# Chunk 2's keys and queries staged during chunk 0's second layer: other rooms, two turns, three loads in flight, chunk norms behind the sums

## The chip, the core and the metric

The kernel runs on one core of a Trainium2 chip. The core has a matrix engine (PE in the profile, its weight loads PEld), three engines for elementwise work (DVE, ACT, POOL), and a sequencer, SP, that does little but issue DMAs. Each engine works through its own list of instructions in order, and waits on semaphores for what other engines or DMAs produce. The metric is the device time of one execution in microseconds (us); lower is better.

## The reference

Inputs are q, k, v of shape (B=4, H=8, S=768, D=48), beta of shape (4, 8, 768), and two weights. Per batch and head a state of 48x48 is carried through the 768 tokens (the delta rule), and the result goes through a two-layer network with SiLU:

```python
k_n = k / (norm(k) + 1e-06)
for t in range(S):
    y[t]  = q[t] @ state
    v_old = k_n[t] @ state
    state = state + beta[t] * outer(k_n[t], v[t] - v_old)
x   = y.transpose(0, 2, 1, 3).reshape(B * S, H * D)      # 3072 x 384
h   = x @ w_in                                           # 384 -> 2048
out = (h * sigmoid(h)) @ w_out                           # 2048 -> 384
```

## The kernel before

**Chunks.** The 768 tokens are cut into 6 chunks of 128 (`NCH`, `C`), and all 32 pairs of batch and head go through a chunk together. Inside a chunk the recurrence becomes a triangular system. For each chunk `c` the kernel makes, in this order:

- `lengths(c)`: the norms of the keys. POOL squares them (`z`, L422), DVE sums the squares (`ss`, L426) and takes a root in a few steps (L441 to L457).
- `load_blocks` (L189): for chunks 2 to 5 it fetches keys and queries from DRAM once more, in blocks of 32 tokens, six DMAs for one half of the batches (G0 or G1) of keys or of queries. `run_rooms` says into which stretch of which other tile: a room that is free at that time. `turn_blocks` (L539, called by `turn_all`) transposes the blocks on DVE into `kq`.
- `spread` (L473, DVE) and `pg` (L496, PE), which put scales of the norms where they are wanted.
- `score` (L580): PE multiplies keys with keys and keys with queries (`pa`), and `ap` takes it out of PSUM, by ACT (L595) and by DVE with a mask (L590). `block_out` and `block_in` take the keys' part of `ap` to DRAM and back in another layout: `blocks<-ap`, then `g<-blocks`.
- `invert(c)`: 31 steps of two instructions on DVE (`rank` L686, `x` L691) and one scaling (L694) invert the 32x32 diagonal blocks. `g<-x`, `low`, `up`, `xe` and `xi` carry the result, partly through DRAM, to `merge` (L840), which puts blocks together on PE (`py`, `px`); `crosses` are its off-diagonal parts.
- `solve(c)`: `ph` (L886, keys on the state), `pz` and `pyc` (L898, L966, L979), `pu` (L918), `state<-state,pu` (L925, DVE). `even_heads` copies the attention's output out of PSUM into `xT`: for odd heads into `part` first, from which DMAs bring it to `xT` (L959).

**The layer.** `xT` is multiplied by `w_in` (`phid`, L1109), goes through SiLU into `gT`, and is multiplied by `w_out`: for chunk 0 by `project` (`po`, L1252, results in `o` and `rest`), for the others by `combine` (`px`/`py`, L1326), which saves products by working on sums of chunks' tiles (`sums_of_g`, L1306, DVE) and of the weights (`sums_of_w`). From chunk 2 on the first product saves some too (`hx`, `hu`, L1163). `run()` issues the next item of the layer.

**What sets the order.** The order on every engine is that of the program text: `pin` ties each instruction to the one pinned before it on its engine, and `in_line` (L104) does so for the DMAs that SP issues. So one waiting instruction holds all that stand behind it on its engine. Ahead of chunk 2 the text is a string of words that `script` reads, one word a step and a number of repeats: `s` a step of `solve`, `r` an item of the layer, `f` a fetch of weights, `t` a step of the sums of `w_out`, `m` a step of chunk 2's norms, `K`, `L`, `y` loads and turns of chunk 2, `c` what is left of chunk 0's layer and the start of chunk 1's. From chunk 2 on, plain loops order the work: `paced` puts steps of `invert` between items of the layer by a balance of estimated times, `run_to` issues items up to a count, and `go(after, n)` puts in n steps of the next chunk's norms.

**Holding back loads.** `linked` lets the first DMA of a call wait for the last one issued ahead of it. `deep(fetch, ..., n=2)` lets each load of a call wait until the n-th load ahead of it has landed, so that n are in flight. `load_blocks` was not called through either.

Of the kernel before, what the change touches and what calls it, by code (L numbers as in the profile page):

```python
# [19 lines left out]
def kernel(  # L20
# [11 lines left out]
    B, H, S, D = q.shape  # L32
    DM, DFF = moe_w_in.shape
    P = 128
# [3 lines left out]
    NP = H // 2  # L38
    BH = B * H
    W = 64  # L40
# [127 lines left out]
    def run_rooms(c):  # L168

        n = HB * NP * RUN  # L170
        ap = ap0s[:].rearrange("p g u h t -> p (g u h t)")
        late = spare_s if c == 2 else halves[int(c == 3)]
        for j, g, of, i in ((0, 0, ap, 0), (0, 1, late, 0), (1, 0, late, 1), (1, 1, halves[0] if c == 2 else ap, 0)):
            runs[c, j, g] = of[:, n * i : n * (i + 1)].rearrange("p (n r) -> p n r", r=RUN)
# [19 lines left out]
    def in_blocks(c):  # L194

        return 1 < c < NCH
# [172 lines left out]
    xis = [xi[:, g] for g in range(2)]  # L369
    crosses = {1: spare_s[:, 0 : HH * T].rearrange("p (n t) -> p n t", t=T)}  # L370

# [662 lines left out]
    def solve(c):  # L1034
# [34 lines left out]
        for hf in range(2):  # L1069
# [7 lines left out]
            for g in range(2):  # L1077
                together(inner(c, g, hf), old(c, g, hf))
            if hf == 1 and c == 1:
                load_blocks(q, 2, G1)  # L1080
            elif hf == 1 and in_blocks(c + 1):
                turn_all(c + 1, 1, G0)
# [212 lines left out]
    def group(g):  # L1295
        return slice(FG * g, min(FG * (g + 1), NFF // 2))

    def sum_g(c, hf, which, fs):
        k, left, right, op = which
        fs = group(fs) if isinstance(fs, int) else fs  # L1300
        of = [
            sums_of_g[:, x, fs] if isinstance(x, int) else
            gT[:, home(c, hf), fs, x[0] * GT + x[1] * C : x[0] * GT + (x[1] + 1) * C]
            for x in (left, right)
        ]
        pin(nc.vector.tensor_tensor(out=sums_of_g[:, k, fs], in0=of[0], in1=of[1], op=op))  # L1306
# [329 lines left out]
    def prepare(c):  # L1636
# [42 lines left out]
    sizes_1 = [0, 1]  # L1679
    sums_made = sum_w()  # L1680
    later = {}

    def script(text):

        nonlocal pieces
        for word in text.split():
# [63 lines left out]
    for text in (  # L1750
        "s f s f T f q T s q T j5 j4 j8 j8 f j5 f q r T j20 j5 j8 j4 j16 j5 j4 b r q r f j4 j4 f W7 r b j4 f2 j4 j4 j32 r f e j6 j6 b j8 j4 f j4 j20 f j4 r j4 j99 l h f2 b l s w2 f r2 l p r s l w3 r p r l p f l2 f l3 b l f l2 s l f l p l3 r l3 s l f l r l2 p f s2 l2 H f l4 f r2 f p2 v l g G r i p i p r2 f i i2 r i r i b l i r f r i r b r2 i b b b i2 r2 i2 f b i5 r6 f r f r i2 r2 f r i r f r f i4 f i b r2 i3 b f b f r i r i f k r f r z i b r s r2 t z s b r2 b s m2 r5 t f t m f t m2 r s t m r b s b m r m2 s K r m L r m r c m2 s y m r m t b m2 s m2 b m f m2 t r t m3 r m s m",
    ):
# [24 lines left out]
    go(after, 99)  # L1777

# [11 lines left out]
    def paced(steps, first):  # L1790
# [81 lines left out]
```

## Time and profile before

| | |
|---|---|
| runs | 649.12, 646.27, 642.19 us; median 646.27 |
| the profiled execution | 653.0 us |
| its span, first to last instruction | 651.3 us |
| mean granted clock of PE | 0.965 of full speed |
| PE busy | 623.3 us (96% of the span) |
| DVE busy | 441.2 us (68%) |
| ACT, POOL busy | 238.8 us (37%), 97.6 us (15%) |
| DMA | 55.07 MB, mean 85 GB/s |

All times of the trace count from the first instruction. The profiled execution is 1.7 us longer than its span, which is what lies around it, and 6.7 us longer than the median of the runs. "Busy" is the time in which an engine works on an instruction. PE's busy time alone doesn't say how much work was done, since the profile also gives the clock that PE was granted, and at half the clock the same products take twice as long. A row of the timeline gives start, duration, engine, line, operation and, in brackets, how long the engine stood idle ahead of it and what ended that. PE's rows in the trace have two records for a product that the program's order has once.

### The profile page before, as it was taken

How to read it: one execution, taken by the hardware profiler on the slowest of the kernel's cores; microseconds unless marked ns; L12 is line 12 of the kernel's file. 1: busy time of each engine (PE TensorE's matmuls, PEld its weight loads, DVE VectorE, ACT ScalarE, POOL GpSimd, SP SyncE). 2: the span in 40 equal slices, each digit the busy share in tenths (PEclk: the TensorE clock that was granted, in tenths of full speed). 3: DMA queues.
4: the chain of work that ended last, by engine and by line, in shares of the span. 5: the costliest groups of instructions: out<-in, count | busy, mean ns of one | idle time of the engine just before them, and what ended most of it. 6: DMA issues, size and time to landing. Idle time of an engine off the chain costs nothing.

```text
span 651.3 us, 21911 instructions
## 1 busy us (share of the span) xinstructions
PE 623.3 (96%) x9570; PEld 544.5 (84%) x9570; DVE 441.2 (68%) x946; ACT 238.8 (37%) x542; POOL 97.6 (15%) x99
## 2 busy tenths in 40 slices
PE   8889899999969998999999999999999999999997
PEld 5678788666658986889898998898998899998997
DVE  5755779998486967577888577986769855231332
ACT  3565655152242122453422443431443324434211
POOL 5433531245000031000050000040000020000000
PEclk9768999999978996999999999999999999999999
DMA  7755554150766129126234546066333060110011
GB/s 152 185 129 170 160 129 98 49 147 3 131 123 123 32 74 173 34 64 129 46 73 78 123 92 134 20 107 130 83 80 73 1 107 13 41 26 0 1 25 25
DMA packets 143936, 55.07 MB, mean 85 GB/s; under 512 B 113488, under 2 KB 137296, under 8 KB 143840
## 3 DMA queue, kind: packets, MB, share of 16 engines
q1 hardware_dynamic: 143360, 53.00, 37.9%
q8 instruction: 75, 1.23, 0.8%
q10 hardware_dynamic: 480, 0.67, 0.4%
q14 instruction: 21, 0.17, 0.1%
HBM read 40.99 MB, written 10.49 MB: 79 GB/s over the span
## 4 chain that ended last, share of the span: by engine, by line
PE 50%; DVE 2%; ACT 1%; POOL 1%; issue 1%; DMA 1%; SPq 0%; DVEq 0%; POOLq 0%; ACTq 0%
PE px L1326 12%; PE hu L1163 12%; PE hx L1163 10%; PE py L1326 9%; PE pz L898 1%; PE ph L886 1%; PE pyc L979 1%; PE pyc L966 1%; PE pa L580 1%; PE pu L918 1%; DVE kq L539 1%; PE py L840 1%; PE px L840 1%; POOL z L422 1%; DMA g<-blocks 1%
## 5 line engine op out<-in xcount | busy, mean ns | idle before, releaser
L1109 PE MATMUL phid<-xT,w_in 128*128 128x256 f32 x384 | 95.7, 403 | 1.0 <-issue 0.9
L1109 PEld LDWEIGHTS phid<-xT,w_in 128*128 128x128 f32 x384 | 74.5, 200 | 13.2 <-issue 2.3
L1326 PE MATMUL px<-sums_of_w,sums_of_g 128*128 128x192 f32 x320 | 57.3, 329 | 1.1 <-DVE sums_of_g L1306 1.1
L1326 PE MATMUL py<-w_out,sums_of_g 128*128 128x192 f32 x320 | 57.4, 329 | 0.0
L1306 DVE TENSOR_TENSOR sums_of_g<-gT 128x512 f32<-128x512 f32 (+2 forms) x44 | 30.7, 734 | 36.9 <-PE py L1326 18.8
L686 DVE SCALAR_TENSOR_TENSOR rank<-g,step,x 128x31 f32<-128x31 f32 (+15 forms) x124 | 49.7, 401 | 7.9 <-DMA g<-blocks 5.0
L1326 PEld LDWEIGHTS px<-sums_of_w,sums_of_g 128*128 128x128 f32 x320 | 52.2, 190 | 2.1 <-ACT o L1367 1.3
L1326 PEld LDWEIGHTS py<-w_out,sums_of_g 128*128 128x128 f32 x320 | 52.2, 190 | 0.5
L1163 PE MATMUL hx<-xT,w_in 128*128 128x256 f32 x192 | 48.0, 379 | 0.0
L691 DVE TENSOR_TENSOR x<-x,rank 128x31 f32<-128x31 f32 (+15 forms) x124 | 42.5, 343 | 4.3
L1163 PE MATMUL hu<-xT,w_in 128*128 128x256 f32 x192 | 45.4, 379 | 0.0
L1163 PEld LDWEIGHTS hu<-xT,w_in 128*128 128x128 f32 x192 | 36.5, 190 | 5.0
L1163 PEld LDWEIGHTS hx<-xT,w_in 128*128 128x128 f32 x192 | 36.4, 190 | 4.8
L1178 DVE TENSOR_TENSOR gT<-gT,hx 128x512 f32<-128x512 f32 x32 | 21.9, 684 | 26.7 <-PE hx L1163 26.4
L1337 DVE TENSOR_TENSOR o<-o,kept 128x192 f32<-128x192 f32 (+1 forms) x29 | 12.4, 426 | 39.8 <-ACT kept L1334 39.4
L580 PE MATMUL pa<-kq 48*64 48x128 f32 (+1 forms) x768 | 26.6, 292 | 6.2 <-ACT xT L595 4.1
L580 PEld LDWEIGHTS pa<-kq 48*64 48x64 f32 x768 | 22.9, 159 | 10.7 <-ACT xT L595 4.9
L595 ACT COPY xT<-pyc 48x128 f32<-48x128 f32 (+2 forms) x120 | 31.1, 259 | 1.6
L925 DVE TENSOR_TENSOR state<-state,pu 48x384 f32<-48x384 f32 x44 | 24.3, 552 | 8.9 <-PE pu L918 7.9
L595 ACT COPY gT<-hu 128x512 f32<-128x512 f32 x32 | 18.7, 585 | 30.6 <-PE hu L1163 30.6
L601 POOL COPY g<-x 64x256 f32<-64x256 f32 x4 | 3.8, 938 | 174.0 <-DVE x L694 174.0
L1326 PE MATMUL py<-w_out,gT 128*128 128x192 f32 x160 | 28.8, 330 | 0.3 <-issue 0.3
(233 smaller groups left out, 1212.6 us busy)
## 6 DMA issues: line engine op xcount, KB each, us to landing
vf<-in_v_dram SPq DMA_DIRECT2D x48, 96.0 KB, 3.7
out_dram<-o SPq DMA_DIRECT2D x42, 96.0 KB, 2.2
w_out<-in_moe_w_in_dram SPq DMA_DIRECT2D x12, 256.0 KB, 3.7
sums_of_w<-in_moe_w_out_dram SPq DMA_DIRECT2D x8, 384.0 KB, 4.2
blocks<-ap SPq DMA_DIRECT2D x40, 64.0 KB, 1.9
g<-blocks SPq DMA_DIRECT2D x4, 512.0 KB
up<-x SPq DMA_DIRECT2D x4, 512.0 KB, 4.2
xi<-up SPq DMA_DIRECT2D x16, 128.0 KB, 3.4
```

The costliest lines, as they stand in the source:

```text
L580: pin(nc.tensor.matmul(pa[e][half, p * n * W : (p + 1) * n * W], lhsT=kq[rows, p, 0, half], rhs=kq[rows, p, js[0] : js[-1] + 1, half], sta ...
L595: return pin(nc.scalar.copy(to, of))
L686: pin(nc.vector.scalar_tensor_tensor(out=tv, in0=g[:, 0:m, m : m + 1].to_broadcast([P, m, n]), scalar=step[:, m : m + 1], in1=x[:, m : m + ...
L691: yield pin(nc.vector.tensor_tensor(out=x[:, 0:m, m:T], in0=x[:, 0:m, m:T], in1=tv, op=ALU.add))
L840: yield pin(nc.tensor.matmul(pm[to, T * n : T * (n + 1)], lhsT=left, rhs=right, start=True, stop=True))
L925: pin(nc.vector.tensor_tensor(out=to, in0=to, in1=by_heads(pu[of]), op=ALU.add))
L1109: pin(nc.tensor.matmul(ph[:, j * GT : (j + 1) * GT], lhsT=w_in[:, a, (2 * f + j) * P : (2 * f + j + 1) * P], rhs=xTs[c, hf][:, a, :], star ...
L1163: pin(nc.tensor.matmul(to[:, GT * i : GT * (i + 1)], lhsT=weights[:, f], rhs=moving, start=start and i == 0, stop=True, skip_group_check=True,
L1178: return lambda: pin(nc.vector.tensor_tensor(out=at(fs, j, hf), in0=at(fs, j, hf), in1=of(room), op=ALU.add))
L1306: pin(nc.vector.tensor_tensor(out=sums_of_g[:, k, fs], in0=of[0], in1=of[1], op=op))
L1326: pin(nc.tensor.matmul(to, lhsT=at, rhs=quarter(f, *b) if isinstance(b, tuple) else sums_of_w[b][:, f], start=start and n == 0, stop=n == ...
L1337: pin(nc.vector.tensor_tensor(out=to, in0=to, in1=of, op=ALU.add))
```

## The change

It has four parts.

1. **Chunk 2's loads.** The keys of the second half of the batches (G1) and the queries of the first (G0) are now fetched (`L`) directly behind the last fetch of `w_out`, the keys of G0 (`K`) and the queries of G1 (the new word `J`, into a room in `sums_of_g` in place of one in `gT`) soon after. All go through `deep(..., n=3)`. The room of `crosses[1]` moves from `spare_s` to `ap0`, behind the runs that lie there.
2. **Turns and scores.** `y1` turns keys and queries of G0, `y2` those of G1. Norms, spread, scores (`P`, `o`), the sums of `w_in` (`u`) and the load of the values (`V`) are now words of the script, the scores with an item of the layer between batches where the words say so.
3. **Invert of chunk 2.** It is no longer issued at a fixed beat but by a balance: each item of the layer gives 1.31 less what DVE's sums beside it take (`spent`), each step takes its estimate. Behind it stand four items ahead of `merge`, where six stood.
4. **The loop over chunks 2 to 5.** The loads of the next chunk's keys (G1) and queries (G0) go three deep, those of chunk 3's keys ahead of the loop. The steps of the norms that stood between `invert` and `merge` are moved: one or three stay there, the others come behind the sums and copies of the following step of `solve`. `paced` begins at the fourth item for each chunk, and `run_to` goes two items further, with fewer behind it.

```diff
...
-        for j, g, of, i in ((0, 0, ap, 0), (0, 1, late, 0), (1, 0, late, 1), (1, 1, halves[0] if c == 2 else ap, 0)):
+        last = sums_of_g[:].rearrange("p k f t -> p (k f t)") if c == 2 else ap
+        for j, g, of, i in ((0, 0, ap, 0), (0, 1, late, 0), (1, 0, late, 1), (1, 1, last, 0)):
...
-    crosses = {1: spare_s[:, 0 : HH * T].rearrange("p (n t) -> p n t", t=T)}
+    behind_runs = ap0s[:].rearrange("p g u h t -> p (g u h t)")[:, HB * NP * RUN :]
...
+    crosses = {1: behind_runs.rearrange("p (n t) -> p n t", t=T)}
...
-            if hf == 1 and c == 1:
-                load_blocks(q, 2, G1)
-            elif hf == 1 and in_blocks(c + 1):
+            if hf == 1 and c > 1 and in_blocks(c + 1):
                 turn_all(c + 1, 1, G0)
...
+        spent[0] += 0.17 + 0.13 * (fs.stop - fs.start)
...
         if in_blocks(c):
-            if c == 2:
-                turn_all(c, 1, G0)
-                yield
-            turn_all(c, 1, G1)
-            if c == 2:
-                yield
+            if c > 2:
+                turn_all(c, 1, G1)
             for b in range(B):
                 scored(b)
+                if c == 2 and b < B - 1:
+                    yield
             block_in(c)
...
             elif what == "K":
-                load_blocks(k, 2, G0)
+                deep(load_blocks, k, 2, G0, n=3)
             elif what == "L":
-                load_blocks(k, 2, G1)
-                load_blocks(q, 2, G0)
+                deep(linked, load_blocks, k, 2, G1, n=3)
+                deep(load_blocks, q, 2, G0, n=3)
+            elif what == "J":
+                deep(load_blocks, q, 2, G1, n=3)
             elif what == "y":
-                turn_all(2, 0, ALL)
+                for j in range(2):
+                    turn_all(2, j, (G0, G1)[n - 1])
+            elif what == "P":
+                later["ready"] = prepare(2)
+                later["step"] = block_steps(2)
+            elif what == "o":
+                go(later["ready"], n)
+            elif what == "u":
+                go(sums_in, n)
+            elif what == "V":
+                linked(load_v, 2)
...
-    ready = prepare(2)
-    go(ready)
-    run(1)
-    go(ready)
-    step = block_steps(2)
-    run(1)
-    go(ready)
-    sums_in = sum_w_in()
-    go(sums_in, 6)
-    linked(load_v, 2)
-    run(7)
-    for n, _ in enumerate(invert(2, step)):
-        run(int(n % 4 != 3 and n != 24))
-        if n == 3:
-            load_k(3)
-    for g in range(2):
-        size(2, g)
-    after = lengths(3)
-    for n in range(6):
-        go(after, 6)
-        run()
-    go(after, 99)
+    assert next(sums_made, 0) == 0
...
+    credit, m, left = 0.0, T - 1, True
+    steps = invert(2, later["step"])
+    while left:
+        spent[0] = 0.0
+        run()
+        credit += 1.31 - spent[0]
+        while left and credit > 0.0:
+            left = next(steps, 0) != 0
+            credit -= 0.38 + 0.00225 * m * (T - m) if m > 0 else 1.2
+            m -= 1
+        if m == T - 6:
+            load_k(3)
+    deep(load_blocks, k, 3, G1, n=3)
+    for g in range(2):
+        size(2, g)
+    after = lengths(3)
+    for n in range(4):
+        run()
+        go(after, (1, 1, 1, 0)[n])
...
-            if n == (1 if c == 2 else 2) and more:
-                assert c == 2 or done[0] >= start(c) - OUTPUT - 4
-                load_blocks(k, c + 1, G1)
-            if n == (2 if c == 2 else 3) and more:
-                load_blocks(q, c + 1, G0)
+            if n == 2 and c > 2 and more:
+                assert done[0] >= start(c) - OUTPUT - 4
+                deep(load_blocks, k, c + 1, G1, n=3)
+            if n == (1 if c == 2 else 3) and more:
+                deep(load_blocks, q, c + 1, G0, n=3)
+            if n > 2:
+                go(after, 8)
             if n == 5 and c == 2:
                 go(sums_in, 2)
+        go(after, 99)
...
-        paced(invert(c + 1, step), 4 if c == 2 else 2)
+        paced(invert(c + 1, step), 4)
...
-        run_to(start(c) + ITEMS + 1)
-        for n in range(7 if c == 2 else 4):
-            go(after, (2, 2, 6, 6, 6, 6, 6)[n])
+        run_to(start(c) + ITEMS + 3)
+        for n in range(3 if c == 2 else 2):
+            go(after, 2 - n)
             run()
-        go(after, 99)
+        go(after, 1)
...
```

The words of the script differ at its end only. From the last `z` on they were, and are now:

```
z i b r s r2 t z s b r2 b s m2 r5 t f t m f t m2 r s t m r b s b m r m2 s K r m L r m r c m2 s y m r m t b m2 s m2 b m f m2 t r t m3 r m s m

z i b r s r2 t z s L b r2 b s K m2 r5 t f t m f t m2 r s J t m r b s b m r m2 s r m r m r c m2 s y1 m t r m b r s m3 b f m2 t r m2 r t m2 s y2 m r m3 s P o2 r u r u r o2 V r3 u4
```

**SP, from the last fetch of `w_out` on.** In the rows `x2` counts equal DMAs in a row; `in_k_dram` and `in_q_dram` are the inputs k and q, `ap_83` is the tile `ap0`, `sums_of_w_in` the room `spare_s`. Before:

```order
L334 DMA sums_of_g<-in_moe_w_out_dram 128x768 x2
L959 DMA xT<-part 48x2x128 x2
L959 DMA xT<-part 16x2x128
L959 DMA xT<-part 32x2x128
L959 DMA xT<-part 48x2x128
L189 DMA ap_83<-in_k_dram 32x8x176
...
L189 DMA sums_of_w_in<-in_q_dram 16x8x160 x2
L104 DMA out_dram<-o 64x384 x4
L104 DMA out_dram<-rest 64x384 x4
L189 DMA gT<-in_q_dram 16x8x176 x2
```

And of the change:

```order
L335 DMA sums_of_g<-in_moe_w_out_dram 128x768 x2
L190 DMA sums_of_w_in<-in_k_dram 16x8x176 x2
...
L190 DMA ap_83<-in_k_dram 16x8x160 x2
L190 DMA sums_of_g<-in_q_dram 16x8x176 x2
L190 DMA sums_of_g<-in_q_dram 16x8x160 x2
L190 DMA sums_of_g<-in_q_dram 32x8x176
L190 DMA sums_of_g<-in_q_dram 32x8x160
L962 DMA xT<-part 48x2x128 x2
L962 DMA xT<-part 16x2x128
L962 DMA xT<-part 32x2x128
L962 DMA xT<-part 48x2x128
L104 DMA out_dram<-o 64x384 x4
L104 DMA out_dram<-rest 64x384 x4
```

All 24 loads now stand ahead of the moves from `part` to `xT`. Before, 18 of them stood between those moves and the stores of `o` and `rest`, and 6 behind the stores.

**PE at the merge of chunk 2.** `phid` is the first product of chunk 1's layer, `py<-xe,ap_83` the merge, `ph` the keys on the state. Before:

```order
L1326 MATMUL py<-w_out_109,sums_of_g 128x192 x4
L1326 MATMUL py<-w_out_110,sums_of_g 128x192 x4
L1109 MATMUL phid<-xT,w_in 128x256 x33
L840 MATMUL py<-xe,ap_83 32x32 x64
L1109 MATMUL phid<-xT,w_in 128x256 x3
```

And of the change:

```order
L1330 MATMUL py<-w_out_109,sums_of_g 128x192 x4
L1330 MATMUL py<-w_out_110,sums_of_g 128x192 x4
L1110 MATMUL phid<-xT,w_in 128x256 x27
L843 MATMUL py<-xe,ap_83 32x32 x64
L1110 MATMUL phid<-xT,w_in 128x256 x3
```

The merge has 27 products ahead of it in place of 33, that is two items of the layer fewer.

**DVE behind the invert of chunk 3.** `x<-x,step` is its last instruction, `sums_of_g<-...` are the sums that `px` and `py` of the layer read, `ss`, `seed` and `nt` belong to chunk 4's norms. Before:

```order
L694 TENSOR_TENSOR x<-x,step 128x1024
L598 COPY g<-x 64x32x24
L1306 TENSOR_TENSOR sums_of_g<-gT 128x512 x2
L426 TENSOR_REDUCE ss<-z 128x8 x4
L441 TENSOR_SCALAR seed<-ss 128x32
L1306 TENSOR_TENSOR sums_of_g<-sums_of_g,gT 128x512 x2
L446 TENSOR_SCALAR nt<-ss,seed 128x32
```

And of the change:

```order
L697 TENSOR_TENSOR x<-x,step 128x1024
L601 COPY g<-x 64x32x24
L1310 TENSOR_TENSOR sums_of_g<-gT 128x512 x2
L1310 TENSOR_TENSOR sums_of_g<-sums_of_g,gT 128x512 x2
L429 TENSOR_REDUCE ss<-z 128x8 x4
L444 TENSOR_SCALAR seed<-ss 128x32
L601 COPY y<-py 32x512 x2
```

The second pair of sums now stands ahead of `ss`, and the root's steps behind the copies of `solve`.

More of the change, by code (lines that the diff above doesn't have):

```diff
@@ L369 @@
     xis = [xi[:, g] for g in range(2)]
-    crosses = {1: spare_s[:, 0 : HH * T].rearrange("p (n t) -> p n t", t=T)}
+    behind_runs = ap0s[:].rearrange("p g u h t -> p (g u h t)")[:, HB * NP * RUN :]
+    assert HB * NP * RUN + HH * T == 2 * HB * H * W
+    crosses = {1: behind_runs.rearrange("p (n t) -> p n t", t=T)}
     ALL_ROWS = slice(0, P)
@@ L1296, in group @@
         return slice(FG * g, min(FG * (g + 1), NFF // 2))
+    spent = [0.0]
     def sum_g(c, hf, which, fs):
@@ L1679 @@
     sizes_1 = [0, 1]
-    sums_made = sum_w()
+    sums_made, sums_in = sum_w(), sum_w_in()
     later = {}
@@ L1750 @@
     for text in (
-        "s f s f T f q T s q T j5 j4 j8 j8 f j5 f q r T j20 j5 j8 j4 j16 j5 j4 b r q r f j4 j4 f W7 r b j4 f2 j4 j4 j32 r f e j6 j6 b j8 j4 f j4 j20 f j4 r j4 j99 l h f2 b l s w2 f r2 l p r s l w3 r p r l p f l2 f l3 b l f l2 s l f l p l3 r l3 s l f l r l2 p f s2 l2 H f l4 f r2 f p2 v l g G r i p i p r2 f i i2 r i r i b l i r f r i r b r2 i b b b i2 r2 i2 f b i5 r6 f r f r i2 r2 f r i r f r f i4 f i b r2 i3 b f b f r i r i f k r f r z i b r s r2 t z s b r2 b s m2 r5 t f t m f t m2 r s t m r b s b m r m2 s K r m L r m r c m2 s y m r m t b m2 s m2 b m f m2 t r t m3 r m s m",
+        "s f s f T f q T s q T j5 j4 j8 j8 f j5 f q r T j20 j5 j8 j4 j16 j5 j4 b r q r f j4 j4 f W7 r b j4 f2 j4 j4 j32 r f e j6 j6 b j8 j4 f j4 j20 f j4 r j4 j99 l h f2 b l s w2 f r2 l p r s l w3 r p r l p f l2 f l3 b l f l2 s l f l p l3 r l3 s l f l r l2 p f s2 l2 H f l4 f r2 f p2 v l g G r i p i p r2 f i i2 r i r i b l i r f r i r b r2 i b b b i2 r2 i2 f b i5 r6 f r f r i2 r2 f r i r f r f i4 f i b r2 i3 b f b f r i r i f k r f r z i b r s r2 t z s L b r2 b s K m2 r5 t f t m f t m2 r s J t m r b s b m r m2 s r m r m r c m2 s y1 m t r m b r s m3 b f m2 t r m2 r t m2 s y2 m r m3 s P o2 r u r u r o2 V r3 u4",
     ):
```

## The prediction

> **What bounds the kernel now.** I read the page's head and first part, then PE's waits, then windows around the largest of them, then the timelines of SP, ACT and DVE there.
>
> ```profile
> span 651.3 us, 21911 instructions
> PE 623.3 (96%) x9570; PEld 544.5 (84%) x9570; DVE 441.2 (68%) x946; ACT 238.8 (37%) x542; POOL 97.6 (15%) x99
> ```
>
> PE is busy in 623.3 of 651.3 us, so 28 us of idle time, and stretches at a reduced clock, are all that an edit of the order can win. PE's waits (us in total, times, longest) say for what it idled:
>
> ```profile
> PE pa L580 <- ACT xT L595: 4.1, 1, 4.1
> PE py L840 <- DMA xe<-low: 2.4, 2, 1.6
> ...
> PE pyc L979 <- issue: 1.6, 2, 1.3
> ...
> PE pg L496 <- DVE spread L473: 1.1, 1, 1.1
> PE px L1326 <- DVE sums_of_g L1306: 1.1, 1, 1.1
> ...
> PE phid L1109 <- issue: 0.9, 2, 0.7
> PE pyc L966 <- issue: 0.9, 1, 0.9
> PE pa L580 <- DVE kq L539: 0.8, 2, 0.5
> PE pa L580 <- DVE ap L590: 0.6, 2, 0.3
> ...
> PE hx L1163 <- DVE gT L1178: 0.4, 1, 0.4
> ```
>
> Two of them are followed by half a clock. In the windows below the columns are stretch, length, busy time of PE, PEld, DVE, ACT, POOL, granted clock, DMA share and GB/s.
>
> ```profile
> 174.14:188.45 14.31, 7.09 (x150) 5.39 (x150) 11.89 (x25) 3.24 (x10) 0.00 (x0) 1.00 0.89 176
> 188.84:199.08 10.24, 10.24 (x133) 8.82 (x126) 7.67 (x16) 4.91 (x16) 1.10 (x2) 0.50 0.44 76
> ...
> 244.16:246.86 2.70, 0.27 (x7) 0.16 (x7) 1.97 (x5) 0.00 (x0) 1.99 (x3) 1.00 1.02 160
> 246.86:257.10 10.24, 10.24 (x260) 8.06 (x264) 7.04 (x27) 1.75 (x3) 0.00 (x0) 0.50 1.03 162
> ```
>
> **Place A**, ahead of chunk 2's scores: PE idles 14.31 - 7.09 = 7.2 us, then works 10.24 us at clock 0.50, which loses 5.1. **Place B**, the merge of chunk 2: 2.4 us idle, then again 10.24 us at 0.50, 5.1 lost. Together 20 us. What makes A wait stands with SP, ACT and DVE:
>
> ```profile
> 137.51 0.82 SPq L334 DMA_DIRECT2D sums_of_g<-in_moe_w_out_dram  x2
> 164.26 3.26 SPq L959 DMA_DIRECT2D xT<-part  x5
> 167.57 2.99 SPq L189 DMA_DIRECT2D ap<-in_k_dram  x6
> ...
> 178.29 3.09 SPq L104 DMA_DIRECT2D out_dram<-o  x4
> 181.47 2.48 SPq L104 DMA_DIRECT2D out_dram<-rest  x4
> ```
> ```profile
> 185.70 1.06 ACT L595 COPY part<-pyc 48x512 f32<-48x512 f32 x2 [9.79 <-DMA out_dram<-rest]
> ```
> ```profile
> 175.48 2.06 DVE L539 STREAM_TRANSPOSE kq<-ap 128x512 f32<-128x512 f32 x2 [5.04 <-DMA sums_of_w_in<-in_k_dram]
> ```
> ```profile
> 188.45 7.03 PE L580 MATMUL pa<-kq 48*64 48x128 f32 x128 [4.14 <-ACT xT L595]
> ```
>
> The 18 loads hold SP from 167.57 to 178.29; behind them stand the stores of `rest`, for whose room ACT's copy into `part` waits until 185.70; `pa` waits for the copies behind that. DVE loses 5.04 us to the same loads, which makes `spread` late for `pg`. SP itself idles from 138.3 to 164.26.
>
> At B the path is a chain off PE:
>
> ```profile
> 199.80 0.34 SPq L104 DMA_DIRECT2D g<-blocks  x1
> ```
> ```profile
> 203.03 0.27 DVE L686 SCALAR_TENSOR_TENSOR rank<-g,step,x 128x31 f32<-128x31 f32 x1 [1.67 <-DMA g<-blocks]
> 237.45 1.22 DVE L694 TENSOR_TENSOR x<-x,step 128x1024 f32<-128x1024 f32 x1
> ```
> ```profile
> 229.75 14.41 PE L1109 MATMUL phid<-xT,w_in 128*128 128x256 f32 x66
> 246.84 1.92 PE L840 MATMUL py<-xe,ap 32*32 32x32 f32 x124 [0.84 <-DMA xe<-low]
> ```
>
> From the end of `pa` (188.45 + 7.03 = 195.48) to the issue of `g<-blocks` are 4.3 us, 3.2 to the first `rank`, 35.6 to the end of `x` (238.67), and 8.17 through DRAM to the merge at 246.84.
>
> **The change, part by part.**
>
> Loads (part 1). None is added; 24 move into SP's idle stretch, and nearly each gets a wait for a landing. Queued behind them on SP are the moves due at 164.26, and `phid` of chunk 1 waits for those. The trace has no `load_blocks` three deep, so I bound it by the landing of the weights' fetch (last number of its row), that of the unheld `load_blocks`, and the twelve three-deep loads of `load_pair` at the start:
>
> ```profile
> sums_of_w<-in_moe_w_out_dram SPq DMA_DIRECT2D x8, 384.0 KB, 4.2
> ```
> ```profile
> DMA to landing us min/median/max: 3.1/3.5/6.1
> ```
> ```profile
> 26.36 7.04 SPq L159 DMA_DIRECT2D gT<-in_k_dram  x6
> 33.90 7.36 SPq L159 DMA_DIRECT2D sums_of_g<-in_q_dram  x6
> ```
>
> From below: 18 unheld loads took (178.29 - 167.57)/18 = 0.60 us each; three in flight with landings of 3.1 would come to 1.03. From above: twelve loads from 26.36 to 41.26 are 1.24 each, in a busier stretch. I take 0.95, nearest to 1.03 and a little under it, since the landings of 3.1 and more are of loads that shared the DMA engines with many others. `linked` starts them when the last fetch has landed, 137.51 + 0.82 + 4.2 = 142.5. They end at 142.5 + 24 x 0.95 = 165.3, so the moves are 1.0 late: **+1.0**. At 0.60 nothing is late; at 1.24 they end at 172.3, 8.0 late.
>
> Place A. With the loads gone the stores follow the moves at about 168, and are done before ACT comes to `part`; it then waits for PE alone, whose `pyc` would end a little over 178 (an estimate from PE's rows without the issue gaps). Taking ACT at 178.75, `pa` can begin 2.75 later, as it did before (185.70 to 188.45): 181.5, its second batch at about 183.1. Turns of G0 (four transposes, 4.1 us) fit where DVE stood idle 5.04 us. About 1.8 of 7.2 us of idle remain, spread over single waits; so the long half-clock stretch should not come. PE would reach the end of chunk 1's first `phid` block 5.4 + 5.1 = 10.5 us earlier.
>
> Place B decides how much of it is kept, because `merge` waits for the chain, not for PE. In the new order three layer items of 1.3 us (3 x 0.43, from 14.41 us over 33 products) stand between the second and third batch's scores: third batch at 184 + 3.9 = 187.9; two batches at full clock take 1.86:
>
> ```profile
> 474.15 3.73 PE L580 MATMUL pa<-kq 48*64 48x128 f32 x128
> ```
>
> so `pa` ends at 189.75. With the spans above: `g<-blocks` 194, first `rank` 197.2. Of the 35.6 us of the invert before, 4.4 were two idle waits:
>
> ```profile
> 207.20 0.56 DVE L1306 TENSOR_TENSOR sums_of_g<-gT 128x384 f32<-128x384 f32 x1 [1.04 <-ACT gT L1117]
> ...
> 212.38 0.43 DVE L1306 TENSOR_TENSOR sums_of_g<-gT 128x256 f32<-128x256 f32 x1 [3.38 <-ACT gT L1117]
> ```
>
> So it takes 31.2 without them and 35.6 with; I take 31.2, since the balance counts the sums (`spent`) before it hands out steps. `x` ends at 228.4, `merge` can begin at 228.4 + 8.2 = 236.6; with 0.3 of rounding, **9.9 us earlier** than 246.84. But two items (six products, 2.6 us) that PE did ahead of the merge now stand behind it, so the net is -9.9 + 2.6 = **-7.3**. PE comes to the merge at 244.2 - 10.5 - 2.6 - 0.5 = 230.6 and idles 6 us there in place of 2.4: A's gain partly turns into B's wait, and B's half clock stays.
>
> [...]
>
> Small terms. The issue gap ahead of `pyc` L966 stood ahead of code now paced otherwise: **-0.9**. The waits of `pa` for `kq` and `ap`, mostly in chunk 3: loads come earlier, **-0.9** of 1.4. Part 4 puts the sums ahead of `ss`; the wait of `px` was this:
>
> ```profile
> 341.82 0.55 DVE L426 TENSOR_REDUCE ss<-z 128x8 f32<-128x384 f32 x1 [0.23 <-POOL z L422]
> ...
> 342.50 1.28 DVE L1306 TENSOR_TENSOR sums_of_g<-sums_of_g,gT 128x512 f32<-128x512 f32 x2
> ```
>
> The sum was ready with 339.5 and stood behind four `ss`: **-1.1**. The later start of `paced` spares `hx` its 0.4: **-0.4**. Issue gaps at the chunks' borders: **-0.6** of the 0.9 at `phid`, where nothing to 0.9 is possible. Against it the later start makes `x` of chunk 4 end later, by an estimated 0.7, and its merge has no slack:
>
> ```profile
> 425.84 1.22 DVE L694 TENSOR_TENSOR x<-x,step 128x1024 f32<-128x1024 f32 x1
> ```
> ```profile
> 436.23 1.37 PE L840 MATMUL py<-xe,ap 32*32 32x32 f32 x128
> ```
>
> From the end of `x` at 427.06 are 9.17 us to the merge, where chunk 2's chain took 8.17 and PE now comes up to two items earlier: **+0.5**. The norms' instructions are as many as before; behind the copies they lie beside `combine`, where DVE has room; without that cover their 4 us of small instructions would come onto `spread`'s path. The moved room of `crosses[1]` costs nothing, as `ap0` is free when the turns have read it.
>
> Sum: -7.3 + 1.0 - 0.9 - 0.9 - 1.1 - 0.4 - 0.6 + 0.5 = **-9.7**. On the profiled execution (653.0, its span and 1.7 us around it) that is 643.3; that execution is 6.7 above the median of the runs, so on 646.27 it is about **636.5**.
>
> **The rivals.**
> - *The chain is shorter than I reckon, and B's wait and half clock vanish as well.* -10.5 at A, -2.4 - 5.1 at B, the rest of the sum -2.4: -20, 626. It needs 6 us less on a chain of 39 whose parts are all measured; that the DMA engines may be less loaded than in B's window (share 1.02) speaks for some of it. 0.10.
> - *Half the way.* A keeps a half-clock stretch, or the invert keeps its 4.4 us of waits, or loads run at about 1.1 us: the chain is 4 to 8 us later, 640 to 646, and all the way to no gain at 647. For it: the clock fell after only 2.4 idle us at B. 0.22.
> - *Slower: three in flight hold SP.* Loads at 1.24 us make the moves 8.0 late; `phid` idles as long and the clock halves (5.1), 13.1 against the 10.7 gained: 649. Each 0.1 us more per load costs 2.4, so from 1.41 on (landings of 4.2; the longest seen is 6.1) it is slower by over 1%: 653, and 656 at 1.55. For it: SP has the moves behind the loads, in order. Against: the median of 3.5. 0.10.
> - *It doesn't do what it says*: the three-deep waits cost, but ACT's wait for the stores goes over to another room. The stores still stand behind the moves; nothing in the order suggests it. Within 0.22 above.
>
> **How the numbers follow.** Forecast 632 to 641: 0.58, around 636.5. The range reaches over the half-way cases to the beginning of the slower one and to the full gain: 626 to 649. A measurement of this kernel tells about 1% (6.5 us) from no change. Faster by more, under 639.8: 0.10 and 0.53 of the forecast's 0.58 = 0.63. Within 1%: the rest of it, 0.05, and 0.20 of the half-way cases = 0.25. Slower: 0.10 and the 0.02 left over: 0.12.
>
> **What would show it.** SP: 24 loads between 142 and 165, the moves at about 165. ACT: no wait of some 10 us for `out_dram<-rest`. PE's clock at 1.00 from 175 to 230. First `rank` of chunk 2 near 197, `x` near 228. PE's largest wait is then the merge's for `xe<-low`, about 6 us near 231, followed by half a clock. `px` no longer waits for `sums_of_g` near 342. I am wrong if the moves start after 168, if the invert begins after 200, or if a gap opens where the trace before has none, above all at the merge of chunk 4.

## The result, and the profile after

| | before | the change |
|---|---|---|
| median of 20 runs each | 648.22 us | 644.95 us |
| ratio to before, with 95% interval | | 0.9944 [0.9918, 0.9969] |
| the profiled execution, its span | 653.0, 651.3 us | 644.67, 642.9 us |
| its mean granted clock | 0.965 | 0.978 |

The change is faster by 0.56%, some 3.6 us, where 9.7 were forecast. Two later comparisons gave 0.992 and 0.9942. The ratios leave out executions that ran slow, by over 1.5%, among them one of the change of 1231.82 us in a later comparison, which nothing here explains. The two profiled executions differ by 8.3 us, more than twice as much as the medians. Below, most events of the prediction are found where it put them; what was wrong is the size of the sum.

The page's head of the change, and PE's longest waits:

```profile
span 642.9 us, 21912 instructions
PE 615.2 (96%) x9570; PEld 538.5 (84%) x9570; DVE 445.9 (69%) x946; ACT 239.2 (37%) x542; POOL 100.5 (16%) x99
```
```profile
PE py L843 <- DMA xe<-low: 6.5, 3, 5.3
...
PE pa L583 <- ACT xT L598: 1.8, 2, 1.2
PE py L1330 <- issue: 1.5, 1, 1.5
PE pz L901 <- DVE vf L894: 1.5, 2, 1.0
...
PE pa L583 <- DVE kq L542: 1.2, 1, 1.2
```

The wait of `pa` at place A went from 4.1 to 1.8 us, those for `xe<-low` grew from 2.4 to 6.5 (6.1 of it at the merge of chunk 2), and there are new ones: `py` (near 346), `pz` behind `vf` (near 262), `pa` behind `kq` (near 372). The prediction had named a gap where the trace before has none as a sign of being wrong, though it looked for it at the merge of chunk 4. PE's busy time fell by 8.1 us though it does the same products (9570 rows in both), with a mean granted clock of 0.978 in place of 0.965: that is the clock.

Windows at place A and place B, columns as in the prediction (length, then busy time of each engine, granted clock, DMA share, GB/s):

```profile
174.14:188.78 14.64, 12.88 (x290) 10.77 (x288) 13.15 (x28) 7.99 (x24) 1.13 (x2) 1.00 0.17 34
229.71:236.17 6.46, 0.32 (x5) 0.19 (x5) 2.21 (x4) 0.00 (x0) 5.71 (x6) 0.71 0.85 187
232.50:242.60 10.10, 6.75 (x198) 5.54 (x198) 4.70 (x8) 1.75 (x3) 2.92 (x4) 0.50 0.85 148
```

At A, PE idles 1.8 us, at full clock. At B it idles 6.1 us, and the half-clock stretch now begins inside the wait: of its 10.1 us only 6.75 fall on work, so it costs 3.4 in this execution, in place of 5.1.

SP's, ACT's and DVE's timelines of the change:

```profile
134.80 0.82 SPq L335 DMA_DIRECT2D sums_of_g<-in_moe_w_out_dram  x2
139.34 5.05 SPq L190 DMA_DIRECT2D sums_of_w_in<-in_k_dram  x6
...
156.55 5.88 SPq L190 DMA_DIRECT2D sums_of_g<-in_q_dram  x6
162.53 3.25 SPq L962 DMA_DIRECT2D xT<-part  x5
...
168.46 3.47 SPq L104 DMA_DIRECT2D out_dram<-rest  x4
```
```profile
177.37 1.06 ACT L598 COPY part<-pyc 48x512 f32<-48x512 f32 x2 [1.24 <-PE pyc L982]
```
```profile
196.57 0.27 DVE L689 SCALAR_TENSOR_TENSOR rank<-g,step,x 128x31 f32<-128x31 f32 x1 [3.04 <-DMA g<-blocks]
...
226.71 1.23 DVE L697 TENSOR_TENSOR x<-x,step 128x1024 f32<-128x1024 f32 x1
```

The 24 loads took 23.1 us, 0.96 each. ACT's copy waits for PE, no longer for the stores. The first `rank` comes at 196.57 and `x` ends at 227.94.

### The profile page after: what moved, and what is told of

The parts are those of the page before. It is cut to its first block, busy times and chain, and to the rows that moved or that the text cites. A ratio compares the mean times of both kernels' runs of the same rounds, so it can differ in the third digit from the quotient of the medians.

```text
span 642.9 us, 21912 instructions
## 1 busy us (share of the span) xinstructions
PE 615.2 (96%) x9570; PEld 538.5 (84%) x9570; DVE 445.9 (69%) x946; ACT 239.2 (37%) x542; POOL 100.5 (16%) x99
## 4 chain that ended last, share of the span: by engine, by line
PE 78%; DVE 10%; DMA 7%; issue 2%; SPq 1%; ACT 1%; POOL 1%; DVEq 0%; POOLq 0%
PE hu L1164 12%; PE px L1330 11%; PE hx L1164 10%; PE phid L1110 10%; PE py L1330 10%; PE po L1253 7%; PE pa L583 3%; PE pz L901 2%; DVE rank L689 2%; DVE x L694 2%; PE ph L889 1%; PE pyc L969 1%; DMA gT<-in_k_dram 1%; PE pu L921 1%; DMA gT<-in_q_dram 1%
## 5 line engine op out<-in xcount | busy, mean ns | idle before, releaser
L1110 PE MATMUL phid<-xT,w_in 128*128 128x256 f32 x384 | 92.6, 394 | 0.8 <-issue 0.7
L1110 PEld LDWEIGHTS phid<-xT,w_in 128*128 128x128 f32 x384 | 72.4, 194 | 12.0 <-issue 1.6
L1310 DVE TENSOR_TENSOR sums_of_g<-gT 128x512 f32<-128x512 f32 (+2 forms) x44 | 33.5, 797 | 25.0 <-PE py L1330 18.8
L1179 DVE TENSOR_TENSOR gT<-gT,hx 128x512 f32<-128x512 f32 x32 | 21.9, 685 | 31.4 <-PE hx L1164 30.7
L901 PEld LDWEIGHTS pz<-vf,xi 64*64 64x64 f32 x768 | 25.5, 142 | 4.9 <-DVE vf L894 2.4
L1164 PE MATMUL hu<-sums_of_g,w_in 128*128 128x256 f32 x128 | 28.9, 379 | 0.0
L901 PE MATMUL pz<-vf,xi 64*64 64x48 f32 x768 | 27.4, 226 | 1.5 <-DVE vf L894 1.5
```

The lines of the kernel that those rows point to most:

```text
L901: yield pin(nc.tensor.matmul(pz[rows, n * D : (n + 1) * D], lhsT=xis[g][rows, u * H + 2 * p + e, :], rhs=vfs[c][rows, hf, g * HB + u, p, : ...
L1110: pin(nc.tensor.matmul(ph[:, j * GT : (j + 1) * GT], lhsT=w_in[:, a, (2 * f + j) * P : (2 * f + j + 1) * P], rhs=xTs[c, hf][:, a, :], star ...
L1164: pin(nc.tensor.matmul(to[:, GT * i : GT * (i + 1)], lhsT=weights[:, f], rhs=moving, start=start and i == 0, stop=True, skip_group_check=True,
L1179: return lambda: pin(nc.vector.tensor_tensor(out=at(fs, j, hf), in0=at(fs, j, hf), in1=of(room), op=ALU.add))
```

## The experiments

All ratios are to the kernel before, on the same chip and run beside it.

### The kernel before, again

No edit. Three more traces of it, the first with timed runs.

> The kernel before, unchanged, to see how its executions differ. In the profiled one the span times the mean clock is 651.3 x 0.965 = 628.5 us, in that of the change 642.9 x 0.978 = 628.8: counted at full clock the two take the same time. Theory 1 (the half-clock stretches differ from execution to execution): spans scatter by 5 us and more, each span times its clock stays at 628 within 2, and a new trace has the same idle time but other half-clock stretches, the one of 6.8 us near 18 us missing in some; the median execution then has a clock near 0.972 and a time of 646 to 649. Theory 2 (the profiled execution had longer waits): span times clock scatters as much as the span, and the clock stays at 0.965.

> The kernel before, unchanged, a third trace. The half clock behind place A took 5.1 us from busy time in the first trace and 2.3 in the second, that behind place B 5.1 in both. Theory (the stretch at A is seldom as long as in the first trace): under 5 at A again, waits at A and B the same within 0.5 us (7.2 and 2.4). Rival (it was a full one and the second trace the exception): 5.1 at A.

> The kernel before, unchanged, a fourth trace; as for the third.

The first gave a median of 645.51 us beside 646.85 for the kernel it was copied from (0.9975 [0.9947, 1.0003]). Over its 12 runs and the 29 of the kernel before, span times clock is 629.2 with a standard deviation of 2.0, the span 644.8 with 2.6, and span and clock go against each other with a correlation of -0.74. So part of the scatter is the clock, as theory 1 has it, but not all: span times clock scatters by 2 too. The mean clock is 0.976, where the profiled execution had 0.965.

To see where, I cut each trace at two events that every kernel here has: the last fetch of `w_out` by SP, and the end of the first products of chunk 2's merge. The cuts are worked out from the timelines, the first row of each group from the fetch to the merge, the last from there to PE's end; rows between them are the stretches at half clock at A and B. First execution (its stretches stand in the prediction), then the second, third and fourth:

```profile
137.95:248.76 110.81, 101.15 (x1498) 82.61 (x1497) 83.03 (x179) 30.46 (x71) 22.42 (x20) 0.95 0.43 85
248.76:647.63 398.87, 394.09 (x5524) 361.68 (x5524) 253.30 (x534) 140.56 (x331) 23.64 (x23) 0.99 0.33 66
```
```profile
133.16:241.81 108.65, 99.21 (x1500) 80.82 (x1498) 82.62 (x178) 30.51 (x71) 22.44 (x20) 0.96 0.42 87
182.40:189.30 6.90, 4.71 (x88) 4.65 (x92) 5.27 (x9) 5.49 (x20) 0.29 (x1) 0.51 0.57 104
240.50:250.70 10.20, 10.20 (x275) 8.03 (x266) 6.76 (x25) 1.75 (x3) 0.00 (x0) 0.50 1.02 169
241.81:639.46 397.65, 393.94 (x5524) 361.71 (x5524) 253.19 (x536) 140.77 (x331) 23.67 (x23) 0.99 0.33 66
```
```profile
136.60:244.28 107.68, 98.81 (x1500) 80.87 (x1498) 82.68 (x177) 30.47 (x71) 22.61 (x20) 0.96 0.41 87
185.50:192.40 6.90, 5.56 (x104) 5.51 (x108) 5.51 (x9) 4.78 (x18) 1.04 (x2) 0.51 0.50 92
243.60:247.00 3.40, 3.40 (x60) 2.39 (x46) 3.07 (x18) 1.15 (x2) 0.00 (x0) 0.50 1.15 154
244.28:641.48 397.20, 392.51 (x5524) 360.33 (x5524) 253.38 (x536) 140.57 (x331) 23.66 (x23) 1.00 0.33 67
```
```profile
134.32:242.02 107.70, 98.52 (x1498) 80.86 (x1497) 82.12 (x175) 30.52 (x71) 22.51 (x20) 0.97 0.41 87
184.30:191.10 6.80, 6.38 (x120) 6.32 (x124) 5.03 (x10) 4.44 (x16) 1.11 (x2) 0.50 0.43 79
242.30:245.70 3.40, 3.40 (x50) 2.48 (x52) 3.05 (x17) 1.57 (x3) 0.00 (x0) 0.50 1.20 186
242.02:637.89 395.87, 391.91 (x5524) 360.10 (x5524) 253.78 (x539) 140.78 (x331) 23.63 (x23) 1.00 0.33 67
```

From fetch to merge the kernel before takes 110.8, 108.7, 107.7 and 107.7 us, 108.7 in the mean. The waits are alike in all four: PE idles 9.7, 9.4, 8.9 and 9.2 us. The half clock isn't: half of the busy time of its rows is what it loses, since the 128 rows of `pa` that took 3.73 us at clock 1.00 (from 474.15) took 7.03 at A, 0.39 of it at 1.00 and 6.64 at 0.50. At A it loses 5.1 in the first execution, 2.4 (4.71/2) in the second, 2.8 in the third, 3.2 in the fourth; at B 5.1, 5.1, 1.7, 1.7. **The execution that I predicted from had the longest stretch at A and one of the two longest at B**, 10.2 us lost where the mean of four is 6.8. Ahead of the fetch, in code that the change doesn't touch, it lost another 10.3, the others 5.7 to 9.2 (mean granted clocks 0.973, 0.976 and 0.981, where it had 0.965). The theory of the third and fourth runs holds.

### The change, again

No edit; twice more.

> The change, unchanged, beside the kernel before on one chip. Theory 1: 0.994 of the time before, clock 0.978 in most executions, span times clock 628 as before; PE's idle time again about 24 us in its longer gaps, 6 of it ahead of the merge of chunk 2, and none ahead of the scores but 1.8. Theory 2: PE's idle time is shorter than before's by some 3.5 us in a new pair of traces.

> The change once more, as one corner of a square of four on one chip: loop new or old, scores and merge as in the change or in one piece with seven items. Theory (part 4 is worth about 1 us in either setting): 1 us faster than with the old loop. Rival (part 4 is worth 3 to 4 us, as predicted): 3 to 4 us faster.

Ratios 0.992 [0.9884, 0.9956] and 0.9942 [0.9912, 0.9973]. The same two stretches of the change, for its first execution and these two:

```profile
135.24:238.09 102.85, 94.57 (x1488) 76.67 (x1486) 82.13 (x170) 30.00 (x70) 22.63 (x20) 0.97 0.42 92
...
238.09:639.23 401.14, 395.38 (x5536) 363.55 (x5536) 259.81 (x543) 141.12 (x332) 26.13 (x23) 0.99 0.32 66
```
```profile
140.26:241.96 101.70, 93.73 (x1486) 76.47 (x1485) 82.02 (x170) 30.02 (x70) 22.50 (x20) 0.97 0.42 93
241.96:640.57 398.61, 394.61 (x5536) 363.31 (x5536) 259.78 (x543) 141.34 (x332) 26.16 (x23) 0.99 0.32 66
```
```profile
133.62:235.28 101.66, 93.81 (x1487) 76.40 (x1485) 82.33 (x170) 30.04 (x70) 22.72 (x20) 0.97 0.41 93
235.28:636.02 400.74, 396.85 (x5537) 364.60 (x5536) 259.86 (x543) 141.33 (x332) 26.16 (x23) 0.99 0.32 66
```

Means: 102.1 from fetch to merge, 400.2 behind it. Against the four traces of before (108.7 and 397.4) that is -6.6 and +2.8, together **-3.8**, which agrees with the ratio (0.56% of 648 is 3.6). Somewhat over half of what the change wins ahead of the merge it keeps; of the 2.8 behind it, 2.6 are the two items that moved there.

The same -3.8 can be split by what PE does. From the fetch to its end PE idles 13.6 us in the mean of the four traces before and 12.6 in the three of the change: the 5.4 us won at A are mostly waited again at B. At A and B together the half clock loses 6.8 before and 4.0 in the change (3.4, 3.4 and 5.2, all at B). That is -1.0 and -2.8, so what the change wins is for the greater part half clock. Theory 1's claim that both kernels take the same time at full clock falls: over all their runs, span times clock is 629 before and 626 in the change.

### The loads back behind the moves

```diff
-... s L b r2 b s K m2 r5 ... m2 r s J t m r b s b m r m2 s r m r m r c m2 s y1 ...
+... s b r2 b s m2 r5 ... m2 r s t m r b s b m r m2 s K r m L r m J r c m2 s y1 ...
```

(and `load_blocks` called without `deep` and `linked`). On the other engines the order is unchanged.

> The change with its 24 loads of chunk 2 back between the moves from part to xT and the stores of o and rest, unheld; only SP's order differs. Theory (where the loads stand on SP makes the wait at place A): ACT's copy into part waits again for out_dram<-rest, until about 187, the scores begin some 9 us later than in the change, the wait ahead of the merge stays at about 6 us, and a half clock follows the scores: 10 to 14 us slower than the change, 653 to 657, slower than the kernel before too, since 6 more loads stand ahead of the stores than there. Rival (the loads' place hardly counts, the gain is from turns and scores in two parts): within 3 us of the change.

655.86 us, 1.0086 [1.0053, 1.012] of before, some 9 us slower than the change (0.9944). ACT's row and PE's two longest waits:

```profile
186.93 1.06 ACT L598 COPY part<-pyc 48x512 f32<-48x512 f32 x2 [11.95 <-DMA out_dram<-rest]
```
```profile
PE pg L499 <- DVE spread L476: 7.1, 1, 7.1
PE py L843 <- DMA xe<-low: 6.4, 3, 5.2
```

The copy waits 11.95 us for the stores again, and `g<-blocks` is issued at 205.33 (193.24 in the change, with the fetch at 134.8 in both). Where the loads stand on SP makes or unmakes place A; turns and scores in two parts without it are worse than the kernel before. The turns on DVE wait for the loads as well, as they did before, here for both parts, the second like this:

```profile
179.57 1.98 DVE L542 STREAM_TRANSPOSE kq<-sums_of_w_in 128x512 f32<-128x512 f32 x2 [4.57 <-DMA sums_of_w_in<-in_q_dram]
```

`spread` stands behind them, and PE's wait for it (7.1 us) is now longer than that for ACT's copies (4.4).

### The loads unheld

```diff
-                deep(linked, load_blocks, k, 2, G1, n=3)
-                deep(load_blocks, q, 2, G0, n=3)
+                linked(load_blocks, k, 2, G1)
+                load_blocks(q, 2, G0)
```

(and the same for `K` and `J`).

> The change with the same 24 loads in the same places, but none held until the third ahead has landed. My prediction put three in flight at 1.0 us of delay of the moves and nothing more. Theory: SP is through with the loads near 155 in place of 162.4, the moves start when part is ready, half a microsecond to 1 earlier, and the time stays within 1 us of the change. Rival (holding the loads spares other DMAs): the loads collide with stores and blocks of chunk 1 between 140 and 160, PE waits there, and it is over 2 us slower.

644.58 us, 0.9937 [0.9906, 0.9968], as the change on other chips. The loads are through at 157.5 in place of 162.4 with the fetch 3.4 us later. Three in flight neither costs nor wins anything here that can be measured.

### Scores of chunk 2 in one piece

```diff
-... s P o2 r u r u r o2 V r3 u4
+... s P o4 V r u r u r4 u4
```

> The change with the four batches of chunk 2's scores in one piece, and the three items that stood between the second and the third batch behind them. Theory (the chain from the scores to the merge sets the end of place B, each microsecond of it counts): the scores end 3 us earlier, with 0.5 to 1 us of wait for the second turns, g<-blocks and the invert start 3 us earlier, the wait ahead of the merge falls from 6.1 to about 3, and the time by 2 to 3 us, to 640 to 642. Rival (the chain waits for something else, DVE or the DRAM, from its start on): the wait stays at 6.

642.66 us, 0.9892 [0.9849, 0.9935], from four executions, beside 644.58 for the unheld loads on the same chip; the intervals overlap.

```profile
PE py L843 <- DMA xe<-low: 4.9, 5, 3.3
```

`g<-blocks` is issued 54.9 us behind the fetch, where the change took 58.0 (193.24 - 135.24), and the longest wait for `xe<-low` falls from 5.3 to 3.3. The chain from the scores to the merge sets the end of place B, as the prediction had it.

### More items ahead of the merge

```diff
-    for n in range(4):
+    for n in range(9):
         run()
-        go(after, (1, 1, 1, 0)[n])
+        go(after, (1, 1, 1, 0, 0, 0, 0, 0, 0)[n])
```

> The change with nine items of the layer in place of four ahead of the merge of chunk 2 (five items of 1.3 us, 6.5 us, are taken from behind it). Theory (the merge waits for its own chain, and the wait of 6.1 us and the half clock behind it are what is left of place B): the wait ahead of the merge falls from 6.1 to under 1 us, no half-clock stretch follows it, and the time falls by 6 to 10 us, to 635 to 639. Rival (the cover is only moved): the scores of chunk 3 now have one item ahead of the invert's first loads in place of six, a wait of 4 to 6 us and a half clock come there, and the time stays within 2 us.

639.63 us, 0.9864 [0.9821, 0.9907]: 2.8 us less than the change on the same chip (642.45), with intervals that overlap a little. The wait at the merge is gone but for 0.5, and more than half of what that should bring comes back behind it:

```profile
PE px L1330 <- issue: 1.7, 2, 1.4
PE pa L583 <- DVE kq L542: 1.7, 1, 1.7
...
PE py L843 <- DMA xe<-low: 0.5, 1, 0.5
```
```profile
277.20:284.00 6.80, 6.62 (x52) 5.78 (x45) 3.09 (x9) 2.12 (x7) 0.00 (x0) 0.50 0.47 80
```

A wait of 1.7 us at chunk 3's scores, which lost five items of cover, was followed by a half clock of 6.8 us. Theory and rival are each right in part.

The same on the kernel before, nine items in place of six:

> The kernel before with nine items of the layer in place of six ahead of the merge of chunk 2, and nothing else. Theory (place B costs its wait of 2.4 us and a half clock of up to 5.1 behind it, by itself and without the loads): the wait is gone, no half clock there, 4 to 7 us faster than before. Rival (a wait of as much comes at chunk 3's scores, which lose three items of cover): within 2 us.

649.29 us, 1.0081 [1.0051, 1.0112]: slower. Here the rival is right, and more than that. The merge's wait was 2.4 us, and three items are 3.9, so the merge itself comes later; then `px` waits 2.1 for issue and `pa` 2.3 for `kq`, and half-clock stretches of 3.4 us (261.40 to 264.90) and 6.8 us (288.80 to 295.60) follow these.

```profile
134.88:246.72 111.84, 104.70 (x1517) 85.36 (x1515) 83.63 (x181) 31.71 (x73) 22.61 (x20) 0.95 0.42 85
246.72:647.14 400.42, 391.27 (x5506) 360.31 (x5506) 251.70 (x533) 139.67 (x329) 23.64 (x23) 0.99 0.32 66
```

With 3.9 us of work moved ahead of it, the part behind the merge should be shorter than 397.4; it is 3.0 longer. (The trace is of an execution of 652.51 us, 3.2 above the median.)

### Both, and the old loop

Scores in one piece and seven items ahead of the merge:

> Scores of chunk 2 in one piece, and seven items of the layer in place of four ahead of the merge: the chain 3 us shorter and 3.9 us more cover, with three items more left to cover chunk 3's scores than with nine. Theory: no wait ahead of the merge over 1 us, the waits of 1.4 near 249 and 1.7 near 275 that nine items brought fall below 1 in sum, and the time is 1 to 3 us below that with nine items (639.6), 637 to 639. Rival (what the cover gives is what the cover can give): the same as with nine items, 639 to 640.

637.71 us, 0.9821 [0.9779, 0.9864]; once more, beside the kernels below, 636.47 us, 0.9853 [0.9815, 0.9892]. This version beats both kernels. In its first trace PE keeps the full clock through places A and B:

```profile
135.46:235.47 100.01, 97.54 (x1506) 79.75 (x1504) 82.54 (x172) 31.17 (x72) 22.71 (x20) 1.00 0.42 93
235.47:630.66 395.19, 389.41 (x5518) 358.52 (x5518) 258.51 (x541) 139.92 (x330) 26.13 (x23) 1.00 0.32 67
```

Part 4 undone, in the change and in this version:

```diff
-                deep(load_blocks, k, c + 1, G1, n=3)
+                load_blocks(k, c + 1, G1)
...
-            if n > 2:
-                go(after, 8)
...
-        go(after, 99)
         go(solving)
...
-        paced(invert(c + 1, step), 4)
+        paced(invert(c + 1, step), 4 if c == 2 else 2)
...
-        run_to(start(c) + ITEMS + 3)
-        for n in range(3 if c == 2 else 2):
-            go(after, 2 - n)
+        run_to(start(c) + ITEMS + 1)
+        for n in range(7 if c == 2 else 4):
+            go(after, (2, 2, 6, 6, 6, 6, 6)[n])
...
```

> The change with the loop over chunks 2 to 5 as before (loads unheld, norms ahead of the merge, paced from the second item, the old counts), the parts ahead of it as in the change. My prediction's small terms: part 4 is worth 3.4 us, so this is 3 to 4 us slower than the change, 648. Rival (what part 4 takes away comes back as other waits: 1.5 ahead of py near 346, 1.2 ahead of the scores near 372, 1.0 ahead of pz near 262): within 1 us of the change.

> Scores in one piece and seven items ahead of the merge, as in the fastest run so far, but the loop over chunks 2 to 5 as before. Theory (part 4 is worth nothing, its waits are exchanged for others): within 1.5 us of the run with part 4 (637.7). Rival (with place B out of the way part 4 shows): 3 to 4 us slower, 641.

The first gave 643.55 us, 0.9962 [0.9929, 0.9994], where the change had 0.992 on the same chip; the second 639.5 us, 0.9918 [0.9891, 0.9946], on another chip than the version with the new loop. Since that left it open what part 4 is worth, the four corners ran once more on one chip:

> The change with the loop as before, beside the change on the same chip. Theory: 1 us slower than the change. Rival: 3 to 4 us slower.

> Scores in one piece, seven items ahead of the merge, new loop. Theory: 4 to 6 us faster than the change, 1 us faster than with the old loop. Rival (with place B gone part 4 shows): 4 us and more faster than with the old loop.

> Scores in one piece, seven items ahead of the merge, old loop. Theory: 1 us slower than with the new loop. Rival: 4 us and more slower.

| | new loop | old loop |
|---|---|---|
| the change | 642.09, 0.9942 [0.9912, 0.9973] | 642.07, 0.9943 [0.9914, 0.9972] |
| scores in one piece, seven items | 636.47, 0.9853 [0.9815, 0.9892] | 638.76, 0.9887 [0.9841, 0.9932] |

In the change part 4 is worth 0.0 us here and 1.1 in the first comparison; in the other version 2.3, with intervals that overlap. The 3 to 4 us of my small terms are not there. A trace of the part behind the merge with the old loop points to why:

```profile
234.83:631.68 396.85, 394.11 (x5536) 362.56 (x5536) 253.33 (x534) 141.19 (x332) 23.65 (x23) 1.00 0.33 67
```

PE idles 396.85 - 394.11 = 2.7 us there, against 5.8, 4.0 and 3.9 in the three traces of the change with the new loop, and 4.8, 3.7, 4.7 and 4.0 in the four of before. Part 4 does take away the wait of `px` for `sums_of_g`, which the old loop keeps (1.1 us), but `pz` behind `vf`, `py` for issue and `pa` behind `kq` cost more than that. This trace is of an execution of 637.1 us, 6.5 below the median of its twelve, so it flatters the old loop. The second trace of the change with the old loop, of 640.28 us, idles 2.4 there. With scores in one piece and seven items the loops idle alike, 5.8 and 5.9 us with the new one, 6.7 and 5.9 with the old. So the exchange of waits is seen in the change alone, and the medians show no gain or loss from it.

## Why the prediction was wrong

Step by step, by its own terms:

- **Loads: right.** 0.95 us each and moves 1.0 late were put; measured 0.96, and the moves start at 162.53 with a fetch 2.7 us earlier, so 1.0 late by the fetch. The 0.95 was a choice between 0.60 and 1.24, not the outcome of a rule. The unheld loads show that this delay costs nothing that can be measured.
- **Place A: the waits right, the half clock over-sized.** Idle time from 7.2 to 1.8 us, as put. By the fetch, `pa` begins at 45.3 where 44.0 was put (180.11 - 134.80, 181.5 - 137.51). The stretch of half clock is gone in the three traces of the change (clock 1.00 from 174.14 to 188.78 in the first), though 1.7 us elsewhere, at chunk 3's scores with nine items, did bring one. It was priced at 5.1, what it cost in one execution; in the three others it took 2.4, 2.8 and 3.2.
- **Place B: right.** The first `rank` comes 61.8 us behind the fetch where 59.7 were put, 1.0 of it by the moves; the invert takes 31.4 us (31.2 put), a wait of 6.1 for 6 put, and the chain decides: one piece of scores shortens wait and time alike. From fetch to merge the forecast was 110.8 - 9.9 + 1.0 = 101.9, and the mean of three is 102.1. The 2.6 of the two items came as put.
- **Small terms: wrong.** -0.9 - 0.9 - 1.1 - 0.4 - 0.6 + 0.5 = -3.4 were put. From the part behind the merge, 400.2 against 397.4 with 2.6 of moved work, they are +0.2. The waits named mostly went, but others as long came in the profiled execution: for the gap at `pyc` (0.9, near 262) that of `pz` (1.0) in the same place, for `px` (1.1) `py` for issue (1.5), for `pa` in chunk 3 (0.8) `pa` near 372 (1.5 with `ap`). I took each removed wait at its full price, and named only one new one. The gap at `pyc` was besides the first execution's own: 0.4 in the third trace of before, and none listed in the second and fourth. The parts moved behind the sums and copies met others there: `pz` waits for `vf`, which on DVE stands behind `spread`, the copies of `n` and the sums of `w_in`:

```profile
260.20 0.39 DVE L476 SCALAR_TENSOR_TENSOR spread<-nr,nt 32x32 f32<-32x32 f32 x2
260.60 0.75 DVE L601 COPY n_slot<-n 64x16 f32<-64x16 f32 x6
261.27 1.28 DVE L1140 TENSOR_TENSOR w_in<-w_in 128x512 f32<-128x512 f32 x2
262.58 1.02 DVE L894 TENSOR_TENSOR vf<-vf,ph 128x384 f32<-128x384 f32 x2
```

- **The base: wrong.** I worked 9.7 us out of an execution that was 6.7 above the median of three runs (4.8 above that of the 20) and took them from the median whole. Of its excess, 2.1 us lay between fetch and merge (110.8 against a mean of 108.7), some 1.7 of it in the half clock at A that the change was to remove (5.1 against a mean of 3.4). A saving that is partly the bad luck of one execution can't be had from the median execution.

These last two make 3.6 + 2.1 = 5.7 of the 5.9 us between -9.7 and -3.8. The rival that came nearest is half the way, though not for its reasons: no half clock was left at A in the traces of the change, and the chain was 1.1 us late beyond the moves in the profiled execution, not 4 to 8.

I took the length of the half clock at B from two rows of 10.24 us, one at A and one at B. Four traces of one wait at B gave two stretches of 10.2 us (5.1 lost) and two of 3.4 (1.7 lost): my rows alone don't give the price.

## What to carry to other kernels

Cut several traces of the same kernel at common events before pricing a stretch of half clock: its length after one and the same wait differed between the four executions of the kernel before (10.2 or 3.4 us at the merge), and the waits hardly did (PE idled 8.9 to 9.7 us from fetch to merge). When a wait on the way to a chain is removed, follow the chain to its end and fill the new wait there, as the scores in one piece and seven items do, but count what cover is left behind: three items too many made the kernel before slower. A list of small waits taken away by reordering an engine came back here as others of the same size; look for the new ones in traces before counting on it.

## What the hardware showed

Stretches at a granted clock of 0.50 lasted 3.4 us (first trace of before, 55.72 to 59.13), 6.8 (the same, 18.17 to 25.00), 10.2 (the same, at both places) or 13.7 (the same, 31.83 to 45.48, and the third trace of the change at B), with PE busy for most or all of each, from 6.75 of 10.10 us to 10.24 of 10.24 (a last one, from 649.64 in the first trace of before, is cut off by the trace's end). At the merge of the kernel before, where PE waited 2.4 us in the first trace, all four traces have one, and so has the change behind 6.1 us (0.50 from 232.37 to 242.61 in its first trace). Waits of 2.3 us (nine items on the kernel before) and 1.7 us (nine items on the change) at chunk 3's scores were followed by one too, of 6.8 us each. Behind the 1.8 us at place A the clock stayed at 1.00, from 174.14 to 188.78 in the first trace of the change and from the fetch to the merge in both traces with scores in one piece and seven items. So one can follow 1.7 us of idle time where 1.8 us elsewhere brought none, and what decides isn't seen here. The stretch that began inside the change's long wait was partly spent on it: with 6.1 us of idle time 6.75 of its 10.10 us fell on work and 3.4 were lost in the first trace. In the third the stretch was longer, 13.7 us, and 5.2 were lost, so in the mean the longer wait lost no less at B than the 2.4 us of before: 4.0 (three traces) and 3.4 (four).

```profile
229.70:243.40 13.70, 10.35 (x248) 8.04 (x252) 5.73 (x10) 1.75 (x3) 3.19 (x5) 0.50 0.84 161
```
